# Sparse attention followed by a gated feed-forward on one core: one order of the same instructions against another, and another rule for products without use

## The chip, the cores and the metric

One NeuronCore of a Trainium2 chip runs the whole program. The metric is device time in microseconds (us), the median of several executions; lower is better. The core has five engines that run side by side, each strictly in its own program order: TensorE (PE, matrix products, with weight loads PEld), VectorE (DVE), ScalarE (ACT), GpSimd (POOL, which here issues the loads) and SyncE (SP, which here issues the stores and the transposes by DMA). They wait for each other, and for DMAs, through semaphores.

## What is computed

Four batches of eight heads, 768 positions, 64 values per head. Every position attends to its neighbours at a distance below 16, and to 24 summaries of blocks of 32 keys (greatest key, mean value):

```python
k_sum = k.reshape(B, H, nb, block, D).max(axis=3)
v_sum = v.reshape(B, H, nb, block, D).mean(axis=3)
scores_l = scale * np.matmul(q, k.transpose(0, 1, 3, 2))
mask_l = np.abs(pos[:, None] - pos[None, :]) < window
scores_s = scale * np.einsum('bhsd,bhnd->bhsn', q, k_sum) + np.log(block)
...
a = np.exp(scores_all)
a = a / (np.sum(a, axis=-1, keepdims=True) + 1e-09)
...
h = x @ w_in
g = h * np.clip(h + 3.0, 0.0, 6.0) / 6.0
return g @ w_out
```

The 3072 rows of attention output x (512 wide) then go through w_in (512 x 2048), the gate, and w_out (2048 x 512).

## The kernel before

Attention goes batch by batch (0 to 3), each in two halves of 384 positions; the feed-forward goes over eight tiles s = 0 to 7 of 384 rows, tile 2b + half from batch b. Feed-forward products of earlier tiles fill PE while the attention of the next batch is prepared.

The program is a list of named operations. The function `op` notes for each its engine, cost, what it reads and writes; `Plan.run` walks through the table ORDER, gives each operation a start time by the costs, lets it take buffers, and sorts by start. So ORDER fixes the order of every engine, and which of two engines (":A" ACT, ":D" DVE) does an operation that either can do. Waits follow from what an operation reads and writes. A name is a tag, a dot and the number of the operation within its tag:

- K0p, Q0.., k0p, q0p: loads of batch 0's keys and queries, then transposes on PE (`k_step`, `q_step`, `q_rest`; L539, L578, L591) and copies on ACT and DVE (L518, L522). Q01w0 to Q01w2 load the second half of the queries.
- s0px: scores of head pair p, half x: a cover product that writes the mask (needs c.4 or n.0), the scores, and the exponential on ACT (L661). s1k, s2k, s3k: the scores of later batches, six groups each, with a mask product on DVE (L692).
- V0c, h0cx: load of the values of pair c, and a copy of the overlap with the neighbouring block (`halo`). In later batches the overlap is loaded (hb0 to hb2).
- u00, u02, u01, u03: sums of values by block on PE (`vsum_first`, L703) and their spread into the value tile (`spread_first`): u00.2 and u01.1 serve half 0 of pairs 0 and 1. The value tile is called vaug.
- v00, v01, v02: values of row tiles 0 to 2 (`values`, `finish`), first pairs 0 and 1 (.0, L814), then 2 and 3 (.1, L816 and L818), reciprocal and scale on DVE (.2 L894, .3 L898), transpose on PE (.4, L911), copy (.5). v00.1 needs h020 and h030. v03: the other half (`values_half`, L845), two groups with reciprocal and scale on DVE, then transposes (.6, .8, .10, L870).
- I0 to I3 and O0 to O3: quarters of w_in and w_out. Fsq: the quarter q of x @ w_in for tile s (L932), the gate on ACT (L938) and DVE (L940), two groups of four operations each; F00 needs I0. Gst: a third t of the product with w_out for tile s (L954), in four groups of four, a copy to one of four ot tiles (.4) and the store on SP (.5).
- Kb, Qb, kb, qb of batches 1 and 2: loads of raw tiles and transposes on DVE (`turn_raw`, L618, L624). wb: greatest keys of blocks (L779) and copies. Batch 3: loads K3., Q3. and transposes by DMA on SP (q3x, k3e); its block sums load v again (B30 to B33, L726, `load_blocks`) into the raw tile of batch 2, and so wait until that has been transposed.
- vb0.6 and vb3.6 for b = 2, 3, and v10.6: the transpose of x by DMA, issued on SP (L858). y10: a copy of two numbers on POOL that waits for v10.6 (L862).
- c.1: the identity, c.2 and c.3: the mask's band, on POOL; c.0, c.4, c.7 to c.9, e, f, n, z: constants on DVE or ACT.

PSUM holds two single banks (h) and three pairs (S) that all products share. POOL's queue is first in, first out: an issue that waits holds up all loads behind it.

At the end, gaps that the plan shows on PE before 27 us (WARM) are filled with products of a constant tile whose results nobody reads (`keep`, L1054), each counted at 0.22 us; how many, the changed line says.

Of the kernel before, what the change touches and what calls it, by code (L numbers as in the profile page):

```python
# [41 lines left out]
F03.3 G02.0 G01.0 k13.0 w1.0 w1.1 F13.0 F13.1 F13.2 F13.3 q12.0 w1.4:A w1.3:A w1.2:A G01.1 G10.0 G10.1 G01.2 G10.2 G11.1
G02.1 G02.2 G10.3 V12.0 V10.0 V13.0 V11.0 q11.0 q13.0 q10.0 q14.0:D G01.3 G01.4:D G02.3 G11.2 G11.3 h100.0:D h121.0:D G02.4:D
G10.4:A h120.0:A h101.0:A h131.0:A c.6:D h111.0:D h110.0:D h130.0:D G11.4:A h21.0 K20.0 Q23.0 K22.0 Q21.0 K21.0 K23.0 K30.0
Q20.0 V23.0 Q22.0 s120.0 s130.0 s110.0 G00.0 G00.1 s130.1 s120.1 s110.1 u1.0 s100.0 s150.0 s140.0 u1.1:A s100.1 s140.1 u1.9:A
G12.0 G00.2 G12.1 s130.2 s120.2 u1.5:D u1.3:D s110.2 s100.2 u1.7:D v13.0 v13.3 u1.8:D v13.1 v13.2 v13.4 v13.5 s140.2 u1.2:A
s150.1 s150.2 u1.6:A u1.4:A G00.3 v13.6 G12.2 G12.3 v13.7:A v13.10 v13.8 v13.11:D v10.3 v10.0 v10.1 v10.4 v10.2 v10.5 G11.5
G02.5 v10.6 v13.9:A F30.0 F30.1 G00.4:A F30.2 F30.4 F30.5 F31.0 F31.1 F30.6 F30.3 k20.0 F30.7 F31.2 F31.3 F33.0 F33.1 F31.4
F31.5 F33.2 F31.6 G12.4:A G10.5 G12.5 G01.5 F33.3 k23.0 F31.7 q22.0 F32.4 F32.5 G32.0 F32.6 F32.7 F33.4 F33.5 F33.6 q21.0
F33.7 F32.0 F32.1 F32.2 F32.3 k22.0 F21.0 G32.1 F21.1 F20.0 F20.1 G31.0 F20.2 q23.0 k21.0 F20.3 q20.0 F21.4 F21.5 F21.6  # L50
# [9 lines left out]
F43.0 F43.1 F43.2 F53.0 F43.3 w3.0 G41.0 F51.0 F53.1 F53.2 F53.3 F51.1 F53.4 F53.5 F51.2 F53.6 G41.1 w3.1 F43.4 F53.7 F51.3  # L60
F43.5 F43.6 F43.7 U3.1 w3.4:D w3.3:D G41.2 F52.0 G40.0 F52.1 G40.1 G41.3 G40.2 G40.3 F52.2 w3.2:D G41.4:D F52.3 G40.4:A
s350.0 s300.0 s320.0 s300.1 s320.1 U3.4:A s350.1 u3.7:A u3.6:A G50.0 G50.1 G52.0 G52.1 s310.0 s340.0 s330.0 G52.2 G52.3 G50.2
s310.1 s340.1 u3.4:A u3.2:A s330.1 u3.0:D s300.2 s350.2 s320.2 u3.1:D s310.2 u3.3:D u3.5:D v33.0 v33.3 G52.4:D G51.0 G51.1
v33.4 v33.1 v33.2 s340.2 v33.5 G42.0 G42.1 G51.2 G51.3 G42.2 s330.2 v30.0 v30.1 v30.2 v30.3 v30.4 v30.5 G42.3 G52.5 G41.5
# [170 lines left out]
def kernel(  # L235
# [814 lines left out]
    def keep(n, o, w):  # L1050
        o = o[:, 0] if any(o is x for x in pairs) else o[:]
        for _ in range(n):
            for lo in range(0, 512, w):
                nc.tensor.matmul(o[:, lo:lo + w], idle[:, 0:128], idle[:, lo:lo + w], start=True, stop=True)  # L1054
# [44 lines left out]
```

## Time and profile before

| what | value |
|---|---|
| median of three runs | 212.79 us (212.48 to 213.14) |
| the profiled execution, first to last instruction (span) | 210.2 us |
| PE busy | 203.4 us (97%) |
| DVE, ACT, POOL busy | 157.8, 111.0, 69.1 us |
| products without use (L1054) | 21 |
| read from memory, written | 30.51 MB, 6.29 MB |

The profile gives no time for the profiled execution as a whole: what lies around its span is taken as the difference to the median. In a row of the timeline stand the start in us, the length, engine, line and operation, the tile written and those read, shapes, a count where rows were merged, and in brackets how long the engine had been idle and what ended that. The ends of PE's rows are modelled and overlap with the next row's start, so products are measured from start to start. In the chain of waits each row is a start, a length and what held the end up then.

### The profile page before, as it was taken

The numbers are of one execution on the slowest core, as the hardware profiler recorded it, in microseconds if no ns is written. First come the engines' busy times: TensorE is split into PE (matmuls) and PEld (weight loads), VectorE is DVE, ScalarE is ACT, GpSimd is POOL, SyncE is SP. The second block draws the span as 40 slices with busy tenths as digits, with TensorE's granted clock in tenths as the row PEclk, the third lists the DMA queues.
The fourth block names the chain that finished last, engine by engine and source line by source line (L and its number), as shares of the span: only waits on it lengthen the run. The fifth ranks groups of instructions, "written<-read, shape, count | busy, mean of one in ns | idle before, by whom it ended". The sixth has DMA issues, their size and how long they took to land.

```text
span 210.2 us, 5069 instructions
## 1 busy us (share of the span) xinstructions
PE 203.4 (97%) x2173; PEld 118.4 (56%) x2173; DVE 157.8 (75%) x241; ACT 111.0 (53%) x158; POOL 69.1 (33%) x84
## 2 busy tenths in 40 slices
PE   7899999999999999999999999999999999999992
PEld 2555878554446695555655466554555555665442
DVE  6879987879998899997499977899473856543222
ACT  5589666554399756365880166451990446613000
POOL 7999424654445606978840000000000000000000
PEclk9999999999999999999999999999999999999999
DMA  4999999999999996999994679900025410001154
GB/s 67 186 154 174 204 202 132 151 150 156 157 126 180 128 111 178 145 163 147 161 168 41 165 138 212 224 3 0 2 78 149 85 43 0 3 0 62 44 189 159
DMA packets 120599, 25.42 MB, mean 121 GB/s; under 512 B 111424, under 2 KB 117440, under 8 KB 120576
## 3 DMA queue, kind: packets, MB, share of 16 engines
q0 software_dynamic: 102656, 15.26, 107.2%
q1 hardware_dynamic: 17920, 9.83, 19.0%
q8 instruction: 17, 0.28, 0.6%
q14 instruction: 6, 0.05, 0.1%
HBM read 30.51 MB, written 6.29 MB: 175 GB/s over the span
## 4 chain that ended last, share of the span: by engine, by line
PE 72%; DMA 8%; DVE 7%; POOL 6%; ACT 2%; issue 1%; SPq 1%; ACTq 0%; DVEq 0%; POOLq 0%
PE S L932 33%; PE h L954 18%; PE S L954 12%; DMA vaug<-in_v_dram 6%; PE S L845 2%; DVE g L940 2%; DVE q L624 2%; POOL nat L448 2%; DMA out_dram<-ot 2%; PE S L684 2%; PE h L1054 1%; PE S L639 1%; POOL vaug L468 1%; DVE qwide L853 1%; DVE kb L618 1%
## 5 line engine op out<-in xcount | busy, mean ns | idle before, releaser
L932 PE MATMUL S<-x,win 128*128 128x384 bf16 (+1 forms) x640 | 88.3, 294 | 0.1
L940 DVE SCALAR_TENSOR_TENSOR g<-r,S 128x768 bf16<-128x768 f32 x64 | 60.1, 948 | 25.6 <-ACT r L938 25.3
L938 ACT ACTIVATE r<-S 128x768 f32<-128x768 f32 x64 | 51.4, 811 | 49.0 <-PE S L932 45.9
L932 PEld LDWEIGHTS <-win 128*128 128x128 bf16 x640 | 54.3, 98 | 30.7 <-issue 0.9
L954 PEld LDWEIGHTS <-g 128*128 128x128 bf16 x416 | 38.7, 98 | 39.9
L954 PE MATMUL h<-wout,g 128*128 128x512 bf16 (+2 forms) x272 | 60.7, 364 | 0.0
L954 PE MATMUL S<-wout,g 128*128 128x512 bf16 (+1 forms) x144 | 30.7, 361 | 0.0
L690 ACT ACTIVATE at<-S 120x1024 bf16<-120x1024 f32 x18 | 17.5, 1022 | 2.5 <-PE S L684 2.4
L468 POOL DMA_DIRECT2D vaug<-in_v_dram x16 | 15.2, 957 | 3.2 <-issue 2.0
L518 ACT COPY ot<-h 128x512 f32<-128x512 f32 (+1 forms) x10 | 5.5, 553 | 18.0 <-PE h L954 18.0
L457 POOL DMA_DIRECT2D nat<-in_q_dram x8 | 10.5, 1315 | 13.1 <-issue 11.2
L457 POOL DMA_DIRECT2D nat<-in_k_dram x8 | 10.7, 1345 | 6.4 <-issue 4.1
L692 DVE TENSOR_TENSOR at<-at,mask 96x1024 bf16<-96x1024 bf16 x18 | 11.7, 682 | 1.0 <-ACT at L690 0.9
L518 DVE COPY ot<-S 128x512 f32<-128x512 f32 x6 | 4.1, 690 | 9.0 <-PE S L954 5.8
L779 DVE TENSOR_REDUCE red<-kb 128x48 bf16<-128x1536 bf16 x6 | 10.4, 1746 | 0.0
L518 ACT COPY ot<-S 128x512 f32<-128x512 f32 (+1 forms) x3 | 1.4, 480 | 16.8 <-DMA out_dram<-ot 9.5
L518 ACT COPY vaug<-vs 24x768 bf16<-24x768 bf16 x10 | 8.2, 828 | 0.2
L522 DVE TENSOR_TENSOR vaug<-vaug 32x768 bf16<-32x768 bf16 (+2 forms) x19 | 6.9, 414 | 1.4 <-DMA vaug<-in_v_dram 1.3
L618 DVE STREAM_TRANSPOSE kb<-nat 128x768 bf16<-128x768 bf16 x8 | 7.7, 964 | 0.0
L1054 PE MATMUL h<-g 128*128 128x512 bf16 x18 | 6.2, 479 | 1.5 <-DVE g L328 1.5
L853 DVE TENSOR_TENSOR xm<-S,rc 128x768 bf16<-128x768 f32 x8 | 7.5, 954 | 0.1
L736 DVE TENSOR_REDUCE total<-nat 128x32 f32<-128x1024 bf16 x4 | 7.6, 1900 | 0.0
(111 smaller groups left out, 172.4 us busy)
## 6 DMA issues: line engine op xcount, KB each, us to landing
out_dram<-ot SPq DMA_DIRECT2D x19, 256.0 KB, 2.6
vaug<-in_v_dram POOLq DMA_DIRECT2D x16, 192.0 KB, 6.5
win<-in_moe_w_in_dram POOLq DMA_DIRECT2D x4, 512.0 KB, 11.2
wout<-in_moe_w_out_dram POOLq DMA_DIRECT2D x4, 512.0 KB, 14.2
nat<-in_k_dram POOLq DMA_DIRECT2D x10, 192.0 KB, 10.1
nat<-in_q_dram POOLq DMA_DIRECT2D x10, 192.0 KB, 11.2
out_dram<-ot SPq DMA_DIRECT2D x4, 224.0 KB, 2.9
nat<-in_k_dram POOLq DMA_DIRECT2D x6, 128.0 KB, 7.0
```

Of the source, the lines that this page charges most:

```text
L457: op("POOL", 1.35, over=0.01, fn=lambda src=src, name=name, hs=hs, ds=ds, rows=rows: nc.gpsimd.dma_start(out=raw[b % 2][name][rows], in_=s ...
L468: op("POOL", 0.945, lambda: nc.gpsimd.dma_start(out=o[BLK:WIN, lo:hi, 0:D], in_=rows[:, lo:hi]), w=[("v", b % 2, c)], dma=1.28, els=1536)
L518: {"ACT": nc.scalar.copy, "DVE": nc.vector.tensor_copy, "POOL": nc.gpsimd.tensor_copy}[eng](o, i)
L618: op("DVE", 0.96, over=0.04, fn=lambda p=p: nc.vector.transpose(out=kb[i][:, :, BLK:WIN].rearrange("x (e u p) c -> x p u e c", e=2, p=NP)[ ...
L690: op("ACT", 1.02, lambda: nc.scalar.activation(odds[0:KEYS, :, w], X.slot[0:KEYS], AF.Exp, scale=scl), r=[X], w=[("atg", k)])
L692: op("DVE", 0.69, lambda: nc.vector.tensor_tensor(odds[0:WIN, :, w].rearrange("p j (t c) -> p j t c", c=QB), odds[0:WIN, :, w].rearrange(" ...
L779: nc.vector.tensor_reduce(red.slot[:].rearrange("x (p u e n) -> x e u p n", p=NP, u=NS, e=2)[:, e], w[:, n * e:n * e + n, BLK:WIN].rearran ...
L853: op("DVE", 0.97, lambda o=o, rc=rc, g=g: nc.vector.tensor_tensor(xm.slot[:, 768 * g:768 * g + 768].rearrange("p (e h d) -> p e h d", e=2, ...
L932: nc.tensor.matmul(h.slot[:, f, u * 128:z * 128].rearrange("p (u c) -> p u c", c=128), w_in_sb[:, kt, (ft + f) * 128:(ft + f + 1) * 128], ...
L938: op("ACT", 0.81, lambda: nc.scalar.activation(r.slot[:], h.slot[:, :, 0:HALF], AF.Relu, bias=0.5, scale=1.0 / 6.0), r=[h], w=[r], alloc=r)
L940: op("DVE", 0.955, lambda: nc.vector.scalar_tensor_tensor(gt[s].slot[:, ft:ft + 2], r.slot[:], 1.0, h.slot[:, :, 0:HALF], op0=ALU.min, op1 ...
L954: nc.tensor.matmul(bank(o)[:, a:z], gt[s].slot[:, ft, ts * 128:(ts + 1) * 128], w_out_sb[:, ft, a:z], start=(ft == 0), stop=(ft == NFT - 1))
```

## The change

ORDER is another one up to F40; from there PE, DVE, ACT and SP have the same order as before, and POOL still has its last loads. No operation is added or taken out. Operations that move from one engine to the other are marked by their letter, such as h020.0 (:D, now :A). In POOL's own order the identity now comes before the band, I1 before I0, I2 before the first raw load of batch 1, and h31, h30 (of batch 3), h20, h21, all V2. and h22 come before the other loads of batch 3, which start with B30; y10 comes after Q31, ahead of V33, h32, V30 and V31 alone. On SP G01.5 moves ahead of v10.6, and G30.5 ahead of v20.6. On DVE the transposes q23, q20 and q22 stand behind w2.0, w2.1 and w2.2.

The rule for the products without use: the margin taken off a gap before it is divided by 0.22 us was 0.15 us up to 16 us and 0.04 us later; it is 0.1 us now.

```diff
-K01.0 K02.0 Q010.0 c.2 Q000.0 c.1 K00.0 Q01w2.0 Q01w1.0 Q01w0.0 k01.0 c.0 z1.0:D c.9 z3.0:D e.2 e.4 e.0 c.7 e.1 z2.0:A z0.0:A
-c.4 e.3 c.8 k03.0 k01.1 k01.4:D k03.1 k02.0 q030.0 s010.0 k01.3:A k01.2:A k03.3:A k02.3:A k03.4:D q030.1:D k03.2:D V00.0
...
-h010.0:D f.0 h031.0:D h030.0:D I0.0 K11.0 I1.0 I2.0 O1.0 I3.0 K13.0 K10.0 K12.0 O0.0 Q11.0 Q12.0 Q13.0 O2.0 Q10.0 O3.0 s031.0
-s021.0 q031.1:A k00.4:A s031.1 s031.2 s021.1 s011.0 s011.1 s021.2 q001.0 s000.0 q001.1:A s000.1 s001.0 s001.1 s011.2 u00.0
-u02.0 s000.2 u01.0:A u00.1:A u00.2:A u01.2:D u01.1:D u02.1:A u03.0:A h020.0:D s001.2 u00.3:A u03.1:A v00.0 v00.1 v02.0 v01.0
-v01.1 v02.1 h021.0:D v00.2 u02.2:D v00.3 v00.4 v01.2 v02.2 v01.3 v02.3 v03.3 v03.0 v03.1 v00.5:A v01.4 v02.4 v01.5:D v02.5:A
-F00.0 F00.1 F00.2 F00.3 F00.4 F00.5 F00.6 v03.2 v03.4 v03.5 v03.6 F00.8 F00.9 F00.10 F00.11 F00.12 F00.13 v03.7:D v03.8 F01.0
...
-G30.0 G31.2 G31.3 G30.1 w2.2:A s240.0 s240.1 G31.4:D s250.0 s230.0 y10.0 h20.0 Q32.0 V30.0 Q33.0 V20.0 V22.0 h22.0 K31.0
...
-Q31.0 V32.0 K34.0 B32.0 B30.0 h32.0 V31.0 Q34.0 Q30.0 V33.0 G21.0 G21.1 G22.2 G22.3 v23.3 v23.0 G20.2 G20.3 G21.2 G21.3 v20.6
-G30.5 G21.4:A U3.2 v23.1 v23.4 U3.3 v23.2 U3.0 v23.5 F40.0 F40.1 F40.2 F41.4 F41.5 F41.6 F40.3 F41.7 G00.5 v23.6 q3x0.0 F41.0
...
+c.0 z3.0:D z0.0:A z2.0:A K01.0 e.1 e.4 e.0 K02.0 Q010.0 c.1 z1.0:D c.2 k01.0 c.8 c.7 Q000.0 k03.0 k02.0 c.4 K00.0 k01.1
+Q01w1.0 s030.0 k01.2:A e.2 Q01w0.0 k01.3:A k03.1 q030.0 Q01w2.0 e.3 q000.0 k02.2:A k03.2:A k03.4:D q030.1:D k02.1 q010.0
...
+s010.1 k02.4:D s010.2 V02.0 k00.3:D k00.1 s020.1 s000.0 q021.0 s021.0 I1.0 I0.0 q021.1:D s020.2 k00.4:D k00.2:A q011.0 s021.1
+s000.1 I2.0 s021.2 q011.1:D q031.0 s000.2 h000.0:A f.0 h001.0:D q001.0 s011.0 s031.0 s011.1 q001.1:D q031.1:D s031.1 h011.0:D
+h010.0:D s001.0 s001.1 K13.0 h030.0:D s011.2 u00.0 h031.0:D s031.2 u01.0:A u00.1:A u00.2:A u02.0 h020.0:A O2.0 u01.1:D
+u00.3:D u02.1:D s001.2 u03.0:D v00.0 v00.1 u03.1:D v00.2 v01.0 v01.1 v00.3 v01.2 u01.2:D I3.0 u02.2:A O0.0 v00.4 v02.0 v01.3
+v02.1 h021.0:A v03.0 v03.3 v00.5:A v02.2 v01.4 K11.0 v02.3 v03.4 v02.4 v03.1 v01.5:D F00.0 F00.1 F00.2 K12.0 F00.3 v02.5:A
+K10.0 v03.2 F00.4 F00.5 v03.6 F01.0 O1.0 F01.1 F00.6 v03.5 F02.0 F01.2 v03.7:D F00.7 v03.10 F02.1 F00.8 F00.9 F01.3 v03.8
...
+s150.1 G00.3 v13.6 u1.6:A v13.7:D u1.4:A s150.2 G12.3 v13.8 v13.10 v13.9:D v10.0 v10.3 v10.1 v10.2 v13.11:A F30.0 v10.4 G11.5
+G01.5 v10.5 Q23.0 F30.1 Q20.0 k22.0 F31.0 F31.1 F30.4 F30.5 F30.2 F31.2 F30.3 F31.3 F31.4 F30.6 F31.5 F30.7 v10.6 F32.4
...
+F21.0 F33.6 F21.1 G32.1 F33.7 F33.2 G31.0 w2.0 G02.5 F20.0 F20.1 F33.3 w2.1 G32.2 F20.4 F20.2 F20.3 F20.5 F20.6 F21.2 G31.1
+G32.3 G32.4:A F23.0 F20.7 F23.1 F23.2 F21.3 w2.4:A F21.4 F21.5 F21.6 h31.0 G31.2 w2.2:D G30.0 w2.3:A G10.5 G31.3 G31.4:A
+h30.0 q23.0 G30.1 q20.0 q22.0 s250.0 h20.0 F21.7 F23.3 s250.1 s240.0 s230.0 h21.0 G30.2 s250.2 V21.0 V22.0 V20.0 G12.5 V23.0
+s240.1 F22.0 F22.1 s230.1 q24.0:D G30.3 h22.0 u2.0 s220.0 s210.0 B30.0 F22.2 F22.3 G30.4:A u2.1:D s200.0 u2.8:D s220.1 s240.2
...
+K32.0 F23.7 v20.0 v20.3 F22.6 s210.2 B31.0 s200.2 v20.1 F22.7 v20.4 v20.2 B33.0 G22.1 v20.5 Q35.0 Q33.0 u2.7:A u2.3:A G30.5
+K30.0 G20.1 G22.2 G22.3 Q30.0 G21.0 u2.9:D v23.3 v23.0 v20.6 G20.2 G21.1 G21.2 K35.0 G21.3 K34.0 K31.0 G20.3 G21.4:A V32.0
+U3.2 v23.1 v23.4 U3.3 Q31.0 v23.2 U3.0 v23.5 F40.0 F40.1 F40.2 F41.4 F41.5 F41.6 y10.0 F40.3 F41.7 G00.5 v23.6 q3x0.0 F41.0
...
+F42.5 F42.6 V33.0 F42.7 F50.0 F50.1 F52.4 F52.5 F50.2 F52.6 F50.3 F52.7 G22.4:D F51.4 F51.5 F50.4 F50.5 F51.6 F51.7 F50.6
+F50.7 F43.0 F43.1 F43.2 F53.0 F43.3 w3.0 G41.0 F51.0 F53.1 F53.2 F53.3 F51.1 F53.4 F53.5 F51.2 F53.6 G41.1 h32.0 w3.1 F43.4
+F53.7 F51.3 F43.5 F43.6 F43.7 U3.1 w3.4:D w3.3:D G41.2 V30.0 F52.0 G40.0 F52.1 G40.1 G41.3 G40.2 V31.0 G40.3 F52.2 w3.2:D
...
-            n = int(max(min(o.begin, SLOW) - end, 0.0) / 0.43 + max(o.begin - (0.15 if o.begin < 16 else 0.04) - max(end, SLOW), 0.0) / 0.22) + (end == BEGIN["PE"])
+            n = int(max(min(o.begin, SLOW) - end, 0.0) / 0.43 + max(o.begin - 0.1 - max(end, SLOW), 0.0) / 0.22) + (end == BEGIN["PE"])
```

More of the change, by code (lines that the diff above doesn't have):

```diff
@@ L29 @@
 ORDER = """
-K01.0 K02.0 Q010.0 c.2 Q000.0 c.1 K00.0 Q01w2.0 Q01w1.0 Q01w0.0 k01.0 c.0 z1.0:D c.9 z3.0:D e.2 e.4 e.0 c.7 e.1 z2.0:A z0.0:A
-c.4 e.3 c.8 k03.0 k01.1 k01.4:D k03.1 k02.0 q030.0 s010.0 k01.3:A k01.2:A k03.3:A k02.3:A k03.4:D q030.1:D k03.2:D V00.0
-q020.0 s020.0 q010.0 q020.1:A q010.1:A c.3 V01.0 V03.0 k02.2:D k02.1 k02.4:D V02.0 k00.0 k00.2:A s010.1 s010.2 q000.0 s030.0
-s030.1 q000.1:A s030.2 k00.1 n.0:D s020.1 s020.2 q011.0 q031.0 q021.0 k00.3:D q011.1:D q021.1:D h001.0:D h000.0:D h011.0:D
@@ L38 @@
-F00.0 F00.1 F00.2 F00.3 F00.4 F00.5 F00.6 v03.2 v03.4 v03.5 v03.6 F00.8 F00.9 F00.10 F00.11 F00.12 F00.13 v03.7:D v03.8 F01.0
-v03.10 F01.1 F00.14 F00.7 F00.15 F02.0 F02.1 v03.11:A v03.9:D F01.2 F02.2 F01.3 F02.3 F10.0 F10.1 F10.2 F10.3 F10.4 F10.5
-F10.6 F10.7 F11.0 F11.1 F11.2 F11.3 F12.4 F12.5 F12.6 F12.7 F03.4 F03.5 F03.6 F03.7 c.5 F01.4 F01.5 F02.4 F02.5 F01.6 F02.6
-F01.7 k12.0 F02.7 F12.0 F12.1 F11.4 F11.5 F11.6 F11.7 F12.2 F13.4 G11.0 F13.5 F13.6 k10.0 F12.3 F13.7 F03.0 F03.1 k11.0 F03.2
@@ L42 @@
[L42 to L50, printed above, removed]
@@ L51 @@
-w2.4:D F21.7 w2.0 G32.2 G32.3 F23.0 F23.1 G31.1 G32.4:A F21.2 F21.3 w2.1 w2.3:D F20.4 F23.2 q24.0:A F20.5 F20.6 F20.7 F23.3
-G30.0 G31.2 G31.3 G30.1 w2.2:A s240.0 s240.1 G31.4:D s250.0 s230.0 y10.0 h20.0 Q32.0 V30.0 Q33.0 V20.0 V22.0 h22.0 K31.0
-h30.0 B33.0 V21.0 G30.2 F22.0 F22.1 s250.1 s230.1 F22.2 F22.3 G30.3 u2.0 s210.0 s220.0 s200.0 G30.4:A s210.1 s240.2 s220.1
-u2.1:D u2.8:D s250.2 s210.2 u2.2:D u2.9:A u2.4:A s230.2 s220.2 u2.7:D G20.0 F22.4 F22.5 F22.6 F23.4 G22.0 F23.5 G20.1 G22.1
-F22.7 u2.3:D u2.6:D F23.6 F23.7 s200.1 v20.0 v20.3 s200.2 v20.4 v20.1 u2.5:D v20.2 v20.5 B31.0 K32.0 Q35.0 h31.0 K35.0 K33.0
@@ L60 @@
[L60 to L64, printed above, removed]
@@ new lines @@
+v02.1 h021.0:A v03.0 v03.3 v00.5:A v02.2 v01.4 K11.0 v02.3 v03.4 v02.4 v03.1 v01.5:D F00.0 F00.1 F00.2 K12.0 F00.3 v02.5:A
+K10.0 v03.2 F00.4 F00.5 v03.6 F01.0 O1.0 F01.1 F00.6 v03.5 F02.0 F01.2 v03.7:D F00.7 v03.10 F02.1 F00.8 F00.9 F01.3 v03.8
+F02.2 Q10.0 F00.10 v03.11:D F00.11 v03.9:D F00.12 F00.13 F00.14 F10.0 F10.1 F02.3 F10.2 F00.15 F11.0 F11.1 F11.2 F02.4 F10.3
+F02.5 F02.6 F10.4 F11.3 F10.5 F12.4 F02.7 F10.6 F12.5 F11.4 F11.5 O3.0 F10.7 F12.6 F12.0 F12.1 F12.7 F11.6 F03.4 F03.5 c.9
+F11.7 F03.0 Q12.0 F12.2 F03.1 F12.3 F01.4 F03.6 F03.7 F01.5 G11.0 F13.4 F01.6 G01.0 k10.0 k13.0 k11.0 F03.2 F13.5 Q13.0 F03.3
@@ new lines @@
+F01.7 Q11.0 k12.0 w1.3:A G11.1 F13.0 F13.1 w1.0 G02.0 F13.2 F13.6 w1.1 G01.1 F13.3 c.5 G02.1 G02.2 w1.2:D w1.4:A F13.7 q11.0
+V10.0 q10.0 G02.3 q12.0 V13.0 G01.2 G10.0 V11.0 G01.3 G02.4:A G01.4:A V12.0 G10.1 q13.0 G10.2 G10.3 c.6:A q14.0:D h131.0:D
+h101.0:A G11.2 h100.0:A G10.4:A s130.0 s110.0 h110.0:A s120.0 s120.1 Q21.0 h130.0:D s130.1 K20.0 s110.1 h120.0:D h121.0:D
+K22.0 h111.0:D G00.0 G11.3 G00.1 u1.0 s100.0 G11.4:A u1.1:A s120.2 s110.2 s100.1 s140.0 u1.9:D s150.0 s130.2 s140.1 G12.0
+Q22.0 G00.2 u1.7:D s100.2 G12.1 K21.0 u1.3:D u1.5:A v13.0 u1.8:A s140.2 v13.1 v13.2 v13.3 v13.4 v13.5 u1.2:A G12.2 K23.0
@@ new lines @@
+h30.0 q23.0 G30.1 q20.0 q22.0 s250.0 h20.0 F21.7 F23.3 s250.1 s240.0 s230.0 h21.0 G30.2 s250.2 V21.0 V22.0 V20.0 G12.5 V23.0
+s240.1 F22.0 F22.1 s230.1 q24.0:D G30.3 h22.0 u2.0 s220.0 s210.0 B30.0 F22.2 F22.3 G30.4:A u2.1:D s200.0 u2.8:D s220.1 s240.2
+G22.0 Q34.0 u2.4:A s200.1 B32.0 s230.2 s220.2 u2.5:D F23.4 F23.5 G20.0 u2.2:D u2.6:D F22.4 F23.6 s210.1 K33.0 F22.5 Q32.0
+K32.0 F23.7 v20.0 v20.3 F22.6 s210.2 B31.0 s200.2 v20.1 F22.7 v20.4 v20.2 B33.0 G22.1 v20.5 Q35.0 Q33.0 u2.7:A u2.3:A G30.5
@@ new lines @@
+F53.7 F51.3 F43.5 F43.6 F43.7 U3.1 w3.4:D w3.3:D G41.2 V30.0 F52.0 G40.0 F52.1 G40.1 G41.3 G40.2 V31.0 G40.3 F52.2 w3.2:D
+G41.4:D F52.3 G40.4:A s350.0 s300.0 s320.0 s300.1 s320.1 U3.4:A s350.1 u3.7:A u3.6:A G50.0 G50.1 G52.0 G52.1 s310.0 s340.0
+s330.0 G52.2 G52.3 G50.2 s310.1 s340.1 u3.4:A u3.2:A s330.1 u3.0:D s300.2 s350.2 s320.2 u3.1:D s310.2 u3.3:D u3.5:D v33.0
+v33.3 G52.4:D G51.0 G51.1 v33.4 v33.1 v33.2 s340.2 v33.5 G42.0 G42.1 G51.2 G51.3 G42.2 s330.2 v30.0 v30.1 v30.2 v30.3 v30.4
+v30.5 G42.3 G52.5 G41.5 G22.5 v33.6 F70.0 F70.1 F70.2 G51.4:A F71.0 F71.1 F71.2 G42.4:D v30.6 G51.5 F70.3 F71.3 F71.4 F71.5
@@ new lines @@
+F71.6 F71.7 F70.4 F70.5 F72.4 F72.5 F70.6 F70.7 F60.0 F60.1 F63.4 F63.5 G50.3 F60.2 F60.3 F63.6 F72.6 F63.7 F61.0 F61.1 F72.7
+G72.0 F61.2 F73.4 F73.5 F73.6 G50.4:A F61.3 F73.7 F72.0 F72.1 F72.2 F72.3 F73.0 F73.1 F63.0 G71.0 F61.4 F63.1 F61.5 F73.2
+F73.3 F63.2 F63.3 G71.3 F61.6 F61.7 F62.4 F62.5 F62.0 G71.1 G71.6 F62.6 F62.7 G71.9 G72.1 G71.4 G72.2 G71.7 F60.4 F62.1
+G71.12 G71.13:A F60.5 G72.3 G70.0 G70.1 G70.2 F60.6 F60.7 F62.2 F62.3 G60.0 G60.1 G70.3 G61.0 G71.14 G42.5 G70.4:D G60.2
+G72.4:D G70.5 G72.5 G60.3 G60.4:D G60.5 G71.10:D G71.11 G40.5 G50.5 G62.0 G62.1 G62.2 G61.1 G61.2 G61.3 G62.3 G61.4:D G61.5
@@ L72 @@
+G62.4:D G62.5 G71.2 G71.5 G71.8 G71.15 G71.16:A G71.17
 """
```

10 lines of the change are left out of this document (2 added, 8 removed).

## The prediction

> **What bounds the kernel now.** I read first the head of the page, then busy time by stretch, cut where the first F product of tile 0 starts (24.78 us), at 60 and at 120.
>
> ```profile
> span 210.2 us, 5069 instructions
> 7.18:24.78 17.60, 16.49 (x392) 11.12 (x392) 15.43 (x39) 15.40 (x33) 16.08 (x19) 1.00 1.96 175
> 24.78:60.00 35.22, 35.22 (x279) 21.73 (x277) 30.70 (x40) 19.66 (x28) 15.83 (x15) 1.00 2.21 159
> 60.00:120.00 60.00, 60.00 (x814) 35.58 (x813) 53.42 (x78) 35.20 (x47) 31.42 (x36) 1.00 2.01 145
> 120.00:206.50 86.50, 86.40 (x667) 47.87 (x665) 53.16 (x69) 37.62 (x49) 0.00 (x0) 1.00 0.31 78
> ```
>
> After each stretch stand its length and the busy time of PE, weight loads, DVE, ACT and POOL, then the granted clock. From 24.78 to the last product PE lacks 0.10 us in 181.7. The change keeps every real product, so the span is the moment at which F00.0 starts, plus a fixed sum of products, plus what PE loses after it. The start and the losses decide.
>
> Here is PE's timeline before F00.0 (start, length, engine, line, tiles, count; weight loads left out), then ACT's and DVE's.
>
> ```profile
> 19.19 0.85 PE L703 MATMUL h<-vaug,ind 96*32 96x128 bf16 x24
> ...
> 20.29 0.32 PE L814 MATMUL S<-vaug,at 120*64 120x65 bf16 x8
> 20.54 0.39 PE L1054 MATMUL h<-g 128*128 128x512 bf16 x1
> 20.86 0.32 PE L816 MATMUL S<-vaug,at 96*64 96x65 bf16 x8
> ...
> 21.35 0.52 PE L814 MATMUL S<-vaug,at 120*64 120x65 bf16 x16
> 21.67 0.32 PE L816 MATMUL S<-vaug,at 96*64 96x65 bf16 x8
> ...
> 22.16 0.53 PE L816 MATMUL S<-vaug,at 96*64 96x65 bf16 x8
> ...
> 23.03 0.40 PE L911 MATMUL h<-ident,xn 128*128 128x128 bf16 x4
> 23.36 1.08 PE L845 MATMUL S<-vaug,at 120*64 120x65 bf16 x48
> 24.37 0.62 PE L911 MATMUL h<-ident,xn 128*128 128x128 bf16 x8
> 24.83 0.39 PE L932 MATMUL S<-x,win 128*128 128x128 bf16 x4
> ```
>
> ```profile
> 19.40 0.83 ACT L518 COPY vaug<-g 24x768 bf16<-24x768 bf16 x1
> ```
>
> ```profile
> 20.19 1.08 DVE L522 TENSOR_TENSOR vaug<-vaug 32x768 bf16<-32x768 bf16 x3
> 21.46 0.21 DVE L894 RECIPROCAL rc<-S 128x8 f32<-128x8 f32 x1 [0.19 <-PE S L818]
> ...
> 22.29 0.69 DVE L898 TENSOR_TENSOR xn<-S,rc 128x512 bf16<-128x512 f32 x1
> ```
>
> u02.0 (19.19) needs the last load of batch 0's V. The issues, as POOL rows, with KB and us to landing under each:
>
> ```profile
> 12.49 0.97 POOL L468 DMA_DIRECT2D vaug<-in_v_dram  x1
> ...
> 13.42 0.82 POOL L503 DMA_DIRECT2D win<-in_moe_w_in_dram  x1
> ```
>
> ```profile
> vaug<-in_v_dram POOLq DMA_DIRECT2D x1, 192.0 KB, 6.6
> ...
> win<-in_moe_w_in_dram POOLq DMA_DIRECT2D x1, 512.0 KB, 8.2
> ```
>
> V02 lands at 12.49 + 6.6 = 19.1, I0 at 13.42 + 8.2 = 21.6: 2.5 us for a quarter of the weights. The order of the loads up to V02 is kept but for the three Q01w among themselves, so **19.1 stays**, however much sooner the scores are done. That anchor carries the forecast.
>
> **The change, part by part.**
>
> *ident before band, scores of pair 3 first, covers earlier.* K01's transposes no longer wait for ident, and ACT begins its copies sooner. All of it lies before 19.1: the work up to s031 gets a lead of some tenths that ends in a longer wait for V02. Price 0; without that cover it could be worth at most what PE lacks there, 17.60 - 16.49 = 1.1 us.
>
> *From V02 to F00.0.* u02.0 starts at 19.19 again, and u00.2 (19.40, 0.83, still ACT's) ends at 20.23, so v00.0 again starts at 20.29. Then three things differ.
> - h020 goes from DVE to ACT, behind u00.2. On DVE it is the first of the three at 20.19 and v00.1 starts at 20.86. On ACT it runs 20.15 to 20.98 (I take the 0.83 of the row above, a copy of like size), so v00.1 starts at 21.05: +0.2.
> - v00.4, the transpose of tile 0, stands right behind v01.1 and ahead of v02. v00.1 takes 21.35 - 20.86 = 0.49 and ends at 21.54; v01.0 takes 0.25 (20.29 to 20.54), v01.1 0.49 (21.67 to 22.16): PE is there at 22.28. DVE's reciprocal and scale of tile 0 run 21.65 to 22.57 (0.12 after v00.1's end, as 21.46 after 21.35; then 0.21 and 0.69, with the gaps). v00.4 starts at 22.62: PE waits 0.34.
> - What follows is v00.4 0.33 (23.03 to 23.36), v02.0 0.25, v02.1 0.49, v03 1.01 (23.36 to 24.37), v01.4 and v02.4 0.46 (24.37 to 24.83): 2.54.
> F00.0: 22.62 + 2.54 = 25.16, against 24.83. **+0.3 us.** v03.6 then follows F00.5 and needs v03.2, which DVE now does behind v03.4, v03.1 and v01.5; this I put inside the 0.3's error. Bounds: with no wait of PE after u02.0 (20.04 at its end, 0.25 + 0.49 + 0.25 + 0.49 + 2.54 of products) 24.1, and with the waits of 0.51 and 0.34 half as long again 25.6: from -0.7 to +0.8.
>
> *I1 ahead of I0.* I0 lands 2.5 later than before, at 24.1, the same moment as the first bound: it costs nothing at 25.16 and takes the bound to about -0.65.
>
> *Fill.* A gap before 16 us now gets a product from 0.32 us on rather than 0.37, one after 16 us only from 0.32 rather than 0.26 (the 0.22 of a product plus the margin). It changes at most one product of 0.22 us per gap. Before 19.1 it lies in PE's slack; after it, one of the two at 19.97 and 20.54 may go, and both stand in waits for ACT and DVE. Price 0, ends -0.2 and +0.2. The granted clock in the first row is 1.00 with 1.1 us of PE idle in it, so there is no clock to win.
>
> *Stores.* G30.5 moves ahead of v20.6 in SP's queue. What it cures is seen in the chain of waits, which there comes to PE out of a store of ot and ACT's copy, and in ACT's row:
>
> ```profile
> 119.90 0.60 ACT ot L518
> ...
> 120.54 3.57 PE S L932 x21
> ```
>
> ```profile
> 119.90 0.59 ACT L518 COPY ot<-S 128x512 f32<-128x512 f32 x1 [9.52 <-DMA out_dram<-ot]
> ```
>
> ACT stood 9.5 us before G21.4 because all four ot tiles were waiting for stores queued behind the x transpose, and F40.2 was queued behind it; PE lost its 0.10 us there. With G30.5 stored first, G21.4 finds a tile. Gain 0.1, or 0.25 if the overlapping ends of PE's rows hide as much again; I take **-0.2**.
>
> *Batch 2 and 3's loads.* y10, POOL's read that waits for batch 1's x transpose, goes from before h20 to behind Q31. In exchange batch 3's other loads hang on B30, which needs DVE to have done batch 2's eight transposes:
>
> ```profile
> 90.81 0.64 POOL L726 DMA_DIRECT2D nat<-in_v_dram  x1 [1.91 <-DVE kb L518]
> ...
> 106.84 0.94 POOL L468 DMA_DIRECT2D vaug<-in_v_dram  x1
> ```
>
> ```profile
> vaug<-in_v_dram POOLq DMA_DIRECT2D x1, 192.0 KB, 5.4
> ```
>
> ```profile
> L940 DVE SCALAR_TENSOR_TENSOR g<-r,S 128x768 bf16<-128x768 f32 x64 | 60.1, 948 | 25.6 <-ACT r L938 25.3
> ...
> L618 DVE STREAM_TRANSPOSE kb<-nat 128x768 bf16<-128x768 bf16 x8 | 7.7, 964 | 0.0
> L779 DVE TENSOR_REDUCE red<-kb 128x48 bf16<-128x1536 bf16 x6 | 10.4, 1746 | 0.0
> ```
>
> Ahead of the last transpose DVE now has two g products more (2 x 0.95), w2.0 and w2.1 (2 x 1.75), and w2.2 in the place of w2.4: 5.4 us, so B30 goes out at 90.81 + 5.4 = 96.2. Behind it POOL has 23 issues at 0.64 to 0.95, some 19 us: the last at about 114 and, with the 5.4 us of the last row, landed at about 120, against 112.2. K and Q are out by then; SP turns them from 123 us on, and V comes last:
>
> ```profile
> 123.06 1.63 SPq L600 DMA_TRANSPOSE q<-nat  x1
> ```
>
> So the lateness is free by itself; its price is what the loads meet, v20.6, below. In the sum it is 0.
>
> Sum: +0.3 - 0.2 = **+0.1 us** on a span of 210.2; around the span lie 212.79 - 210.2 = 2.6 us, taken as unchanged. 212.79 + 0.1 = 212.9.
>
> **The rivals.** *Slower: the x transpose of v20.6 meets the late loads.*
>
> ```profile
> 79.98 0.17 POOL L862 COPY seen<-x 1x2 bf16<-1x2 bf16 x1 [8.27 <-DMA x<-xm]
> ```
>
> ```profile
> 114.02 1.29 SPq L858 DMA_TRANSPOSE x<-qwide  x1
> ```
>
> ```profile
> x<-xm SPq DMA_TRANSPOSE x1, 4.8
> ...
> x<-qwide SPq DMA_TRANSPOSE x1, 4.2
> ```
>
> ```profile
> 119.00 8.20 PE L932 MATMUL S<-x,win 128*128 128x384 bf16 x48
> ```
>
> y10 held POOL for 8.27 us, until batch 1's x transpose had landed; v20.6 (114.02) had no such guard and needed none: with all loads landed (112.2) it took 4.2 us, and F40.0 at 119.00 had 0.8 to spare. Batch 1's, at the end of a row of loads, took 4.8. In the new order v20.0 stands two G groups sooner, 2 x 0.86:
>
> ```profile
> 43.52 0.86 PE h L954 x4
> ```
>
> That gives its issue at 114.0 - 1.7 + 0.3 (PE's own lateness) = 112.6; F22.7's g product now lies among v20's scalings, so I say 112.9. F40.0 comes at 119.3, so 6.4 us may pass. Among loads to 120 us, at an even share of the DMA engines, it takes 2 x 4.2 = 8.4: PE stands 2.0 us. This decides as soon as the transpose takes over 6.4. Time: 212.9 + 2.0 = 214.9. Against it: 4.8 is all that the one meeting here cost. The Trainium skill ("DMA: Bandwidth & Descriptors", Issuing engines are not separate DMA queues, with the arbitration in Queues, rings and completion order) says that DMAs of all issuers share the same 16 engines and that these go round the queues packet by packet; by that rule the even share, and so 214.9, is what to expect; no row here has a transpose amid a full backlog.
>
> *Faster: the wait at V02 shrinks.* If DVE and ACT keep ahead after u02.0, F00.0 starts as I0 lands: -0.65, with the stall -0.85: 211.9. For it: DVE has idle time in the first stretch (15.43 of 17.60). Against: h020 is last on ACT. No gain beyond this is open, since PE is full from there on.
>
> *Slower: DVE late at batch 2.* w2.2 and three transposes, 0.5 + 3 x 0.96 = 3.4 us, stand in a row ahead of F21.7 and F23.3, which free S pairs for s240 and s230. PE's cover is four G groups, G31.2 to G30.1, 4 x 0.86 = 3.4, and what DVE is ahead by. If DVE comes there a microsecond late, PE waits for as long: 213.9.
>
> *It changes nothing:* the lead ends at V02 and nothing else shows. That is the forecast but for its two small terms.
>
> **How the numbers follow.** Forecast and its neighbourhood (F00.0 between -0.2 and +0.8) 0.45; faster start 0.20; transpose among loads 0.23; late DVE 0.12. This kernel can't tell less than about 0.3% (0.64 us) from no change. The first case stays inside 212.15 to 213.43, its own range being 212.4 to 213.4; the second lies below; the last two above. So faster 0.20, same 0.45, slower 0.35. The range runs from the faster rival's 211.9 to the transpose's 214.9.
>
> **What would show it.** Right: u02.0 near 19.2 and F00.0 near 25.1, v00.4 waiting for DVE; B30 issued near 96; no ACT wait on a store before F40. Wrong: F00.0 by 24.3; PE idle just ahead of F40.0 with x as the releaser; PE gaps at s240 or s230; V02 landing elsewhere than at 19.1.

## The result and the profile after

The changed kernel takes 220.38 us (median of four, 219.41 to 220.98) against 212.89 (212.48 to 213.14): a ratio of 1.0355, 95% interval 1.0322 to 1.0388. That is 7.5 us slower, outside the range. The profiled execution took 220.52 us, 0.14 from the median. Now and then an execution of a kernel falls into a slower state; medians and ratios here and below are over the others.

| what | before | after |
|---|---|---|
| span | 210.2 us | 218.8 us |
| mean granted clock of TensorE | 0.998 | 0.984 |
| first product of F00.0 | 24.83 | 24.77 |
| first product of F40.0 | 119.00 | 125.13 |
| from there to the end of the span | 91.2 | 93.7 |

The start is the same to 0.06 us. Of the 8.6 us, 6.2 are lost between F00.0 and F40.0, and 2.5 behind F40.0, where PE's products are the same ones in the same order. First the head of the page after and its clock by fortieths of the span:

```profile
span 218.8 us, 5050 instructions
...
PE 204.4 (93%) x2154; PEld 119.5 (55%) x2178; DVE 155.2 (71%) x240; ACT 112.8 (52%) x159; POOL 69.4 (32%) x84
...
PEclk9999999999999999999999859999999999999999
```

PE is busy as long as before (203.4) in a longer span, so it stood; and there is one dip of the clock, at slices 23 and 24. Where PE stood, by PE's waits (what it waited for; us in total, times, longest) and PE's timeline at the same places:

```profile
PE S L932 <- DMA x<-qwide: 4.0, 1, 4.0
...
PE S L932 <- DMA x<-xm: 1.3, 1, 1.3
PE S L932 <- DMA win<-in_moe_w_in_dram: 0.6, 1, 0.6
```

```profile
28.42 0.82 PE L932 MATMUL S<-x,win 128*128 128x384 bf16 x4 [0.62 <-DMA win<-in_moe_w_in_dram]
...
86.10 1.47 PE L932 MATMUL S<-x,win 128*128 128x384 bf16 x8 [1.25 <-DMA x<-xm]
...
125.13 15.11 PE L932 MATMUL S<-x,win 128*128 128x384 bf16 x75 [4.02 <-DMA x<-qwide]
```

Three waits, all for DMAs and together 5.9 of the 6.2 us: the third quarter of w_in, batch 1's x transpose (v10.6, ahead of F21) and batch 2's (v20.6, ahead of F40). None of them is in the profile before. The rest of the loss is the clock. In the busy time by stretch (length; PE, PEld, DVE, ACT, POOL; then clock, DMA share, GB/s):

```profile
115.00:120.00 5.00, 4.84 (x67) 2.62 (x67) 4.92 (x6) 0.00 (x0) 1.95 (x3) 1.00 2.15 153
120.00:125.00 5.00, 1.11 (x6) 0.29 (x3) 2.35 (x2) 0.58 (x1) 0.00 (x0) 0.89 2.28 163
125.00:130.00 5.00, 4.87 (x16) 2.28 (x17) 0.95 (x1) 0.81 (x1) 0.00 (x0) 0.50 1.34 185
130.00:135.00 5.00, 5.00 (x30) 2.90 (x29) 2.78 (x3) 3.32 (x5) 0.00 (x0) 0.93 1.00 213
```

For the five us behind the wait TensorE ran at half clock: it is busy, but does 16 products where it does 33 at full clock, and 2.5 us of work are missing.

Now the two transposes on SP's queue, their issue (start, length) and, from the view of DMA issues, the us from issue to landing:

```profile
75.45 2.80 SPq L858 DMA_TRANSPOSE x<-xm  x1
...
114.35 2.12 SPq L858 DMA_TRANSPOSE x<-qwide  x1
```

```profile
x<-xm SPq DMA_TRANSPOSE x1, 10.6
...
x<-qwide SPq DMA_TRANSPOSE x1, 10.7
```

They were issued within half a microsecond of before's times (75.01 and 114.02). What changed is how long they take: 10.6 us instead of 4.8, and 10.7 instead of 4.2. And POOL's rows:

```profile
73.75 3.68 POOL L491 DMA_DIRECT2D vaug<-in_v_dram  x4 [6.09 <-PE S L845]
77.42 3.75 POOL L468 DMA_DIRECT2D vaug<-in_v_dram  x4
...
97.87 0.61 POOL L726 DMA_DIRECT2D nat<-in_v_dram  x1 [10.64 <-DVE q L624]
...
113.41 0.17 POOL L862 COPY seen<-x 1x2 bf16<-1x2 bf16 x1
...
115.39 1.87 POOL L468 DMA_DIRECT2D vaug<-in_v_dram  x2 [0.31 <-DMA nat<-in_q_dram]
```

Eight loads from v (four of the overlaps, L491, and four of V, L468) go out right around the transpose issued at 75.45; before, y10 held them back until it had landed. POOL then stands 10.64 us ahead of B30 (issued 90.81 before) until DVE has done batch 2's transposes, and the last load goes out at 116.3 instead of 106.84: the transpose issued at 114.35 lies amid the loads.

### The profile page after: what moved, and what is told of

Read it like the earlier page. It is cut to its first block, busy times and chain, and to the rows that moved or that the text cites. A ratio compares the mean times of both kernels' runs of the same rounds, so it can differ in the third digit from the quotient of the medians.

```text
span 218.8 us, 5050 instructions
## 1 busy us (share of the span) xinstructions
PE 204.4 (93%) x2154; PEld 119.5 (55%) x2178; DVE 155.2 (71%) x240; ACT 112.8 (52%) x159; POOL 69.4 (32%) x84
## 4 chain that ended last, share of the span: by engine, by line
PE 69%; DMA 16%; POOL 6%; DVE 4%; issue 2%; ACT 1%; DVEq 0%; SPq 0%; ACTq 0%; POOLq 0%
PE S L932 33%; PE h L954 20%; PE S L954 11%; DMA win<-in_moe_w_in_dram 6%; DMA x<-qwide 5%; DMA x<-xm 5%; POOL vaug L468 2%; PE S L845 2%; PE S L684 2%; DVE at L692 1%; DVE g L940 1%; POOL qwide L435 1%; POOL nat L415 1%; ACT at L690 1%; DVE vaug L518 1%
## 5 line engine op out<-in xcount | busy, mean ns | idle before, releaser
L932 PE MATMUL S<-x,win 128*128 128x384 bf16 (+1 forms) x640 | 91.0, 299 | 5.9 <-DMA x<-qwide 4.0
L932 PEld LDWEIGHTS <-win 128*128 128x128 bf16 x640 | 55.0, 99 | 38.8 <-DMA x<-qwide 4.5
L954 PE MATMUL h<-wout,g 128*128 128x512 bf16 (+2 forms) x254 | 58.1, 362 | 1.7 <-issue 1.3
L518 ACT COPY ot<-h 128x512 f32<-128x512 f32 (+1 forms) x12 | 6.7, 559 | 19.6 <-PE h L954 19.6
L468 POOL DMA_DIRECT2D vaug<-in_v_dram x16 | 15.1, 950 | 0.8 <-issue 0.5
L457 POOL DMA_DIRECT2D nat<-in_q_dram x8 | 10.5, 1316 | 13.4 <-issue 9.5
L518 ACT COPY vaug<-vs 24x768 bf16<-24x768 bf16 x12 | 9.8, 828 | 0.2
L518 DVE COPY ot<-S 128x512 f32<-128x512 f32 x5 | 3.4, 690 | 9.0 <-PE S L954 6.7
L1054 PE MATMUL h<-g 128*128 128x512 bf16 x22 | 7.5, 458 | 1.8 <-DVE g L328 1.5
L518 ACT COPY ot<-S 128x512 f32<-128x512 f32 (+1 forms) x4 | 2.0, 506 | 13.8 <-PE S L954 13.8
L624 DVE STREAM_TRANSPOSE q<-nat 128x768 bf16<-128x768 bf16 x8 | 7.2, 950 | 0.9 <-DMA nat<-in_q_dram 0.9
```

Source lines behind the costliest of these rows:

```text
L457: op("POOL", 1.35, over=0.01, fn=lambda src=src, name=name, hs=hs, ds=ds, rows=rows: nc.gpsimd.dma_start(out=raw[b % 2][name][rows], in_=s ...
L468: op("POOL", 0.945, lambda: nc.gpsimd.dma_start(out=o[BLK:WIN, lo:hi, 0:D], in_=rows[:, lo:hi]), w=[("v", b % 2, c)], dma=1.28, els=1536)
L518: {"ACT": nc.scalar.copy, "DVE": nc.vector.tensor_copy, "POOL": nc.gpsimd.tensor_copy}[eng](o, i)
L932: nc.tensor.matmul(h.slot[:, f, u * 128:z * 128].rearrange("p (u c) -> p u c", c=128), w_in_sb[:, kt, (ft + f) * 128:(ft + f + 1) * 128], ...
L954: nc.tensor.matmul(bank(o)[:, a:z], gt[s].slot[:, ft, ts * 128:(ts + 1) * 128], w_out_sb[:, ft, a:z], start=(ft == 0), stop=(ft == NFT - 1))
```

## The experiments

Theory A: a transpose by DMA that meets loads takes 10 to 11 us instead of 4 to 5, and that is the loss. Rivals in the expectations: B, the transposes are late because they are issued late; C and D, the quarters of w_in land later when a raw load follows them, or when three of them stand in a row. In the diffs "..." leaves out what lies between the places in ORDER.

**e1: the guard alone goes back.**

```diff
-F21.6 h31.0 G31.2
...
-F41.6 y10.0 F40.3
+F21.6 y10.0 h31.0 G31.2
...
+F41.6 F40.3
```

> The changed kernel with one step undone: y10, POOL's wait for batch 1's x transpose, stands ahead of h31 again, so that no load of batch 2's values is issued until that transpose has landed. Theory A (meeting): an x transpose that shares the DMA engines with a running row of loads takes 10 to 11 us instead of 4 to 5. Then v10.6 lands 4 to 5 us after its issue, the 1.4 us that PE lost ahead of F21 are gone, and the wait ahead of F40, whose transpose still meets batch 3's loads, stays at 3 to 5 us: span 218.8 - 1.4 = 217.4, time about 219.0. Theory B (late issue): the transposes are slow or late for a reason on SP or DVE, and POOL's loads have no part in it: v10.6 still takes over 10 us and the span stays at 218.8.

Measured: 218.66 us (218.09 to 219.62), ratio 1.0284 (1.0241 to 1.0328). The transpose of v10.6 in the DMA view, and all waits of PE for x:

```profile
x<-xm SPq DMA_TRANSPOSE x1, 3.8
```

```profile
PE S L932 <- DMA x<-qwide: 4.0, 1, 4.0
```

It lands in 3.8 us, the wait ahead of F21 is gone, 1.7 us come back, and F40's wait stays. Nothing else was moved, so the guard was what kept v10.6 short. The 1.7 us are not the guard's alone: three of e1's four executions have a mean clock of 0.991 or 0.992, where all four of the changed kernel have 0.984.

**e2: the late loads go early**, with y10 left where the change put it.

```diff
-h22.0 u2.0
+h22.0 Q34.0 K33.0 Q32.0 K32.0 Q35.0 Q33.0 K30.0 Q30.0 K35.0 K34.0 K31.0 Q31.0 V32.0 V33.0 h32.0 V30.0 V31.0 u2.0
```

(The same names are taken out further on, so that B30 to B33 come last on POOL.)

> The changed kernel with POOL's order of batch 3's loads turned round: K3., Q3., V3. and h32, which wait for nothing of batch 2, go right behind h22, and B30 to B33, which wait for DVE's last transpose of batch 2, go last (S pairs rotate otherwise from F33 on). Theory A: POOL's loads then end before v20.6 is issued, it lands about 4.2 us after its issue as in the kernel before, the 4.2 us ahead of F40 and the stretch at half clock behind it (about 2.7 us) go, and F21's 1.4 us and F02's 0.8 us stay: span 218.8 - 6.9 = 211.9, time about 213.6. Theory B: v20.6 still takes over 10 us, span near 218.8. If the half clock has another cause than the wait, the span is near 214.6.

Measured: 212.94 us (212.18 to 213.71), ratio 0.9998 (0.9969 to 1.0027): the whole loss is gone, although v10.6, still without its guard, took 9.9 us there. In the profile of e2, the wait for x, the landing and the stretch that had the half clock:

```profile
PE S L932 <- DMA x<-xm: 0.5, 1, 0.5
```

```profile
x<-qwide SPq DMA_TRANSPOSE x1, 3.7
```

```profile
125.00:130.00 5.00, 5.00 (x33) 3.00 (x31) 3.79 (x4) 3.59 (x5) 0.00 (x0) 1.00 1.03 206
```

Issued at 113.42, 0.9 earlier than in the changed kernel, v20.6 lands after 3.7 us, as all loads had landed (113.4). B can account for those 0.9 us, not for the 7 that the transposition itself became shorter. The clock is full again without anything done to it.

**e3: e1 and e2 together; e4: e3 with K13 behind I3.**

> The two edits before this one together. Theory A: both waits for x and the half clock are gone, only F02's wait for I2 (0.8 us) is left: span 218.8 - 1.4 - 6.9 = 210.5, time about 212.2, the same as the kernel before within what can be told. Theory B: 218.8.

> As the run before, and K13, the raw load behind I2, goes behind I3, so that a weight load follows I2. Theory C: a weight load that is followed by a raw load of many short packets lands later, because the raw load's packets run ahead on some of the 16 engines: I2 then lands near 26.6 and F02 does not wait: span 210.5 - 0.8 = 209.7, time about 211.4, 0.7% below the kernel before. Rival D: I2 is late because three weight loads in a row take longer than 2.5 us each; then it still lands near 28 and the span stays near 210.5.

Both missed: e3 1.0111 (1.0028 to 1.0194, from two executions), some 215 us, and e4 1.0075 (1.004 to 1.011), some 214.4. Of e3 there is no profile that can be compared, so e4 has to speak for both. Its x transposes took 3.8 and 5.6 us, as A has it. Most of the loss is a new wait (its profiled span is 3.4 us longer than before's; the start gives the rest, with 1.6 us of waiting for the first keys and F00.0 at 25.89); VectorE's timeline and PE's wait in e4:

```profile
117.78 1.92 DVE L736 TENSOR_REDUCE total<-nat 128x32 f32<-128x1024 bf16 x1 [4.05 <-DMA nat<-in_v_dram]
...
121.59 0.95 DVE L853 TENSOR_TENSOR xm<-S,rc 128x768 bf16<-128x768 f32 x1
```

```profile
PE S L932 <- DVE xm L853: 2.5, 2, 1.3
```

With the guard in, POOL's loads start some 5 us later (h22 at 92.06 instead of 86.28), and B30 to B33, put last, are the ones that come too late: DVE's block sums wait 4.05 us for them and hold up the scaling of v23 behind them. C and D find no support: the third quarter of w_in landed at 26.54 with K13 moved, and at 26.63 in e1 and 26.91 in e2 with the changed order of loads. Of the traces of the changed order, only the changed kernel's own had it at 28.38, and only there PE waited for it.

**e5: the guard, and the block loads in the middle.** As e3, with B32, B33, B30 and B31 behind Q33, the sixth of the early loads.

> The guard of x<-xm back ahead of the loads, the loads of q, k and v for the last stage early, and batch 3's block loads (B30 to B33) behind the sixth of them instead of last, where VectorE waited for them in e4 (4.05 us at the first block sum, 2.5 us on TensorE for xm). Theory A (only the meetings of a transpose with loads and the late block loads cost time): x<-xm takes 3.8 us, x<-qwide 4 to 6, the block loads land by 106, no wait for xm on TensorE; span 210.5 to 211.2, time 212.0 to 213.0. Rival (with the guard in, GpSimd has some 5 us less for its loads, and something at the end of batch 2 is late whichever load goes last): 214 to 216, with a new wait of TensorE between 113 and 130 us.

Measured: 212.26 us (ratio 0.9974, 0.995 to 0.9998). The wait for xm is gone. The profiled execution was one of its longer ones (213.98 us, span 212.3), and the reason is the mechanism again:

```profile
PE S L932 <- DMA x<-qwide: 1.3, 2, 0.9
```

There the last load landed at 119.67, and v20.6, issued at 113.48, took 7.4 us. The rival (something is late whichever load goes last) is wrong by the median, 212.26 against its 214 to 216.

**e7: the kernel before without its guard.** The other direction: in the old order y10 alone goes from ahead of h20 to behind V33.

> The kernel before with one edit: y10, the guard of x<-xm, at the end of GpSimd's order, so that loads are issued while the transpose waits for its turn. Theory A (a transpose that meets loads takes 10 to 11 us): x<-xm goes from 4.8 us to about 10, and TensorE waits 0.5 to 2 us ahead of F21, as it did in the changed kernel (1.4); on the other side GpSimd's later loads come some 5 us sooner, which is worth little here; 213.5 to 214.5. Rival (it is the changed order about it that makes the transpose slow): 4 to 5 us as before, and a time within 0.5 us of 212.8.

Measured: ratio 1.0063 (1.003 to 1.0096), 1.3 us slower. PE's timeline and the DMA view:

```profile
86.13 0.82 PE L932 MATMUL S<-x,win 128*128 128x384 bf16 x4 [1.27 <-DMA x<-xm]
```

```profile
x<-xm SPq DMA_TRANSPOSE x1, 10.5
```

With nothing of the change in it, the same transpose takes 10.5 us once loads are issued beside it. The 4.8 us of before are the guard's work.

**e8: products in the wait.** The changed kernel with products that nobody reads ahead of F40:

```diff
+if s == 4 and ft + f == 0:
+    for _ in range(20):
+        nc.tensor.matmul(h.slot[:, 1], w_in_sb[:, 0, 0:128], w_in_sb[:, 0, 0:512], start=True, stop=True)
 for kt in range(NP):
```

> The changed kernel with 20 products of 512 columns more, whose results nobody reads, ahead of F40, where TensorE stood for 4.2 us. If the half clock behind that wait comes from the standing still: the row of 125 to 130 us shows a clock near 1.00 instead of 0.50, the wait is filled, and the time falls by about 2.7 us to 217.7. If the half clock has another cause (the load of the phase itself): the clock there stays near 0.50 and the time stays at 220.4, or rises by what the products take beyond the wait.

Measured: 218.17 us (ratio 1.0249, 1.0218 to 1.028), 2.2 us less than the changed kernel. PE's timeline and the stretch (three lines were added, so L932 is L935):

```profile
121.13 4.48 PE L933 MATMUL S<-win 128*128 128x512 bf16 x20
125.57 10.72 PE L935 MATMUL S<-x,win 128*128 128x384 bf16 x65
```

```profile
125.00:130.00 5.00, 5.00 (x31) 2.88 (x30) 1.69 (x2) 1.96 (x3) 0.00 (x0) 1.00 1.81 136
```

F40 starts 0.4 later than in the changed kernel, for the same transpose, yet from there to the end of the span it is 216.5 - 125.57 = 90.9 us against 93.7, and 91.2 before. Standing still costs the clock: 2.5 to 2.8 us on top of the wait of 4.0.

**e9: the new rule for products without use, in the old order.** One line differs from before, and one product without use is left out, the one at 20 us.

> The kernel before with the change's second part alone: products without use fill shorter gaps too, in the old order. Theory A (the fill is not part of the loss): 212.8, at most 0.4 away. Rival (more products without use hold TensorE up at the start, or draw the clock down): 213.3 or more, with F00 later than 24.9 us or a mean clock under 0.995.

Measured: ratio 1.0023 (0.9999 to 1.0047), too little to be told from none, but not evenly spread: five of ten executions had a mean clock of 0.99 and took 213.58 to 214.18, the other five 212.54 to 213.29 at 0.997 or more. The kernel before has such executions too, but fewer: six of the 78 beside these experiments (0.989 to 0.992, 214.24 to 214.67 us). The profiled one of e9 is of the first kind:

```profile
23.00:25.00 2.00, 2.00 (x53) 1.66 (x55) 1.85 (x5) 1.09 (x2) 0.84 (x2) 0.64 1.24 205
25.00:27.00 2.00, 2.00 (x32) 1.94 (x29) 1.23 (x3) 0.57 (x1) 0.93 (x1) 0.50 1.25 213
```

At about 23.6 us the clock falls to half until 27, and F00.0 starts at 26.18. The changed kernel and the others in its order showed nothing of the kind at the start.

**e10: the store of G30.5 ahead of v20.6 on SP, in the old order.**

> The kernel before with one edit: the store of G30.5 goes ahead of the transpose v20.6 in SyncE's queue. The prediction's term says that ScalarE's wait of 9.5 us ahead of G21.4 goes away and that the time falls by 0.1 to 0.25 us, too little to be told from none: 212.6, at most 0.3 away. Rival (the transpose, now queued behind the store, comes later and TensorE waits for it): x<-qwide issued 1 us or more later than 114.0, a wait ahead of F40, 213.5 or more.

Measured: 213.13 us, ratio 0.9999 (0.9977 to 1.0022). ACT's row of copies from S has lost its 9.5 us of waiting for a store. TensorE waits 0.4 us for x, but so it does in e9, where the store was not moved, so this wait is not shown to be the store's doing:

```profile
L518 ACT COPY ot<-S 128x512 f32<-128x512 f32 (+1 forms) x3 | 1.4, 480 | 16.3 <-PE S L954 16.3
```

```profile
PE S L932 <- DMA x<-qwide: 0.4, 1, 0.4
```

**e6: the new order up to F00.0, the old one behind it.**

> The changed order up to F00.0 (and the new rule for products without use), the old order for all that comes behind it. If the changed start is worth nothing (the prediction's anchor, V02's landing, holds, with the 0.3 us of v00.4's wait measured at 0 in the changed kernel): F00.0 near 24.8, time 212.8, at most 0.4 away. If the changed start is itself a gain that the loss at batch 2 hides: 212.3 or less. If it costs the 0.3 us that the prediction put on it, or makes the first weights late: 213.1 or more.

Measured: 215.97 us, ratio 1.0132 (1.0108 to 1.0156), more than any of the three answers had. The two halves don't fit, as VectorE's timeline shows:

```profile
44.52 0.98 DVE L618 STREAM_TRANSPOSE kb<-nat 128x768 bf16<-128x768 bf16 x1 [2.14 <-DMA nat<-in_k_dram]
```

The new start loads batch 1's keys later, the old rest turns them at the old moment: DVE stands 2.14 us, and PE 1.95 behind it. So e6 says nothing about what the start is worth.

**e11 and e12: filling POOL's idle time in e5.**

> e5 with one edit: h22, the last piece of a tile whose earlier pieces must have landed, goes behind the first six loads of q and k. In e5 GpSimd stood from 87.6 to 92.3 us for it, and the last load landed at 119.67, so x<-qwide (issued 113.48) still took 7.4 us in the profiled execution. Theory A: with that hole filled the last load lands near 115, x<-qwide takes 3.7 to 5.5 us, TensorE does not wait for it; span 210.0 to 210.9, time 211.7 to 212.4. Rival (GpSimd's hole is no loss, the DMA engines were the limit there: the loads land as late as in e5): last landing 118 to 120, time as e5's, 212.26, at most 0.2 away.

Measured: 232.7 us, ratio 1.093 (1.0901 to 1.0959). The edit moved more than was meant: V20 to V23 stand between h21 and h22 in ORDER and so came last of all loads, and the sums over batch 2's values stood for them:

```profile
PE h L749 <- DMA vaug<-in_v_dram: 18.5, 2, 17.5
```

e12 leaves V20 to V23 in place; Q34, K33, Q32, K32, Q35 and Q33 go ahead of h22, and K30, Q30, K35 and K34 ahead of the block loads.

> What e11 was to test, with batch 2's own loads of V left where they are: against e5, the first six loads of q and k of the last stage go ahead of h22, and four more ahead of the block loads, so that GpSimd does not stand while h22's earlier pieces land (in e5 from 87.6 to 92.3 us). Theory A (a transpose pays for the loads that it meets): the last load lands at 114 to 116 instead of 119.67, x<-qwide (issued near 113.5) takes 3.7 to 5.5 us instead of 7.4, TensorE does not wait for it; span 210.0 to 210.9, time 211.7 to 212.3. Rival (the DMA engines are the limit there and GpSimd's hole is no loss): last landing 118 to 120, x<-qwide 6 us or more, time 212.3 or more.

Measured: 212.52 us against 213.00 in the same series, ratio 0.9973 (0.9949 to 0.9997). In its DMA view:

```profile
x<-qwide SPq DMA_TRANSPOSE x1, 5.3
```

The last load landed at 117.35, between A's 114 to 116 and the rival's 118 to 120: by one trace of each kernel, filling the hole gained half of what was expected, and in time nothing over e5. Both kernels stand 0.5 us below the kernel before, each with an interval that ends just short of 1, at the limit of what can be told. They are the only two that do, and what in the changed order gives the half microsecond was not found.

## Why the prediction was wrong, by its own steps

- **The loads of batches 2 and 3: "In the sum it is 0".** This is the step that failed. The lateness itself was forecast well for the issues (B30 at 97.87 for 96.2, the last at 116.3 for about 114), less so for the last landing (127.3 for about 120); its price was not. It measured 4.0 us of waiting ahead of F40 and 2.5 us of half clock behind it, 6.5 of the 8.6 us; with the loads early, e2 has neither.
- **Batch 1's x transpose had no price at all.** I read 4.8 us as what a meeting with loads costs ("4.8 is all that the one meeting here cost"). But in that row the guard, removed by the change, kept the meeting short. e7 shows the row without its protection: 10.5 us. Price: the 1.3 us ahead of F21, which the guard takes away in e1.
- **The rival of v20.6 was the right mechanism, with a chance of 0.23 and 2.0 us.** Two sizes were off. The transpose takes 10.7 us among loads, not the even share of 8.4. With 6.8 us from its issue (114.35) to PE's arrival at F40 (some 121.1; forecast 6.4), that makes 4.0 instead of 2.0. And the half clock behind the wait, 2.5 us, was no term of the sum; e8, where products fill the wait, shows that it follows from the standing still.
- The Trainium skill ("DMA: Bandwidth & Descriptors", Queues, rings and completion order) has the engines go round the queues packet by packet, from which I worked out the 8.4. The packets of the two queues do run side by side in the trace (last section); the time does not come out at the even share: 9.9 (e2), 10.5 (e7), 10.6 and 10.7, up to 11.4 (e8). The Trainium skill ("TensorE: Matmul & The Clock Gate", What's actually happening) says that an idle window of about 3.4 us takes the clock to half; the trace agrees with it in the 0.50 behind 4.0 us, and in the full clock behind 1.3. The half clock of e9, with no such wait, it does not explain.
- **The start.** Forecast: u02.0 anchored at V02's landing, then +0.3. From u02.0 to F00.0 it went from 19.19 to 24.83, 5.64 us, before, and from 18.92 to 24.77, 5.85, after: +0.2, near the forecast. v00.4 waited for DVE as forecast (the scale ends at 22.21, v00.4 starts at 22.27); a product without use fills part of that wait, so that it stands in no list of waits. The anchor is no anchor. In e10, with the old order, V02 landed at 18.80, sooner than before's 19.13, and u02.0 started at 19.68, later: PE came there with its own work. In the traces of the changed order that start lies anywhere from 18.92 to 20.36, and F00.0 from 24.77 to 26.22, so the 0.2 can't be seen in a time; that both profiles compared above start F00.0 at 24.8 is luck.
- **The store of G30.5 (-0.2).** ACT's wait went away as forecast, here and in e10. Whether the 0.2 us came can't be told: e10's interval is 0.5 us wide to either side.
- **The fill (0, from -0.2 to +0.2).** Perhaps too narrow: with one product left out, e9 has five executions of ten that are 1 us longer by the clock, the kernel before six of 78. In the changed order it cost nothing that shows.
- **DVE late at batch 2.** Right to give it a small chance: no wait of PE ahead of s240 or s230.

Shown by edits in both directions: what v10.6 loses by meeting loads (e1 and e7). Shown in one direction, by taking the cause away: the same for v20.6 (e2, and e4, e5 and e12 with fewer loads in the way) and the clock's part (e8, e2). Seen once and left open: the 0.6 us for the third quarter of w_in, which no repeat of that order showed.
